# Attention on one Trainium2 core: the weights times the values in float32 on two column groups, and U^T x of the token mixing once per batch

## The chip, the cores and the metric

The kernel runs on one core of one Trainium2 chip. Its time is the device time of the whole program in microseconds (us). Five engines work side by side, each with a queue of its own that runs in order: TensorE (PE in the profile, with PEld for the loading of its weights), VectorE (DVE), ScalarE (ACT), GpSimd (POOL) and SyncE (SP, which here only issues DMAs). The kernel before takes 675.28 us, the median of three runs (675.28 to 675.33).

## The reference

Three stages, all in float32. Only the first two bear on the change.

```
q, k, v: (2, 8, 768, 64)   batch, heads, tokens, head dimension
mask   = q_assign[:, :, :, None] == k_assign[:, :, None, :]      # nearest of 16 centroids
scores = where(mask, q k^T / 8, -1e9)
attn   = exp(scores - max) / sum                                 # (768 x 768) per head
x      = attn @ v, heads side by side                            # (2, 768, 512)

h  = x^T @ U @ V            # U: 768 x 32, V: 32 x 768: mixes the tokens
u  = x + h^T
x  = u + relu(u @ w_ch1) @ w_ch2                                 # 512 -> 2048 -> 512
out = gated convolution block (512 -> 1024 -> 512)
```

## The kernel before

**Attention.** There are 2 x 8 heads of 6 row tiles of 128 tokens: 96 tiles, n = 0 to 95. `step(n)` (L666) writes out by hand what each engine does in one step; the order of the calls is the order in the queues, since the schedule is manual. In a step, three tiles are in work at once:

- PE: `s_mm(n + 2)` makes the scores of tile n + 2, 128 x 768, in PSUM (`sc`, L369 and L380, four matmuls). Then `pv_mm` (L431), then `t_mm(n)` transposes the finished weights `e` of tile n in six 128 x 128 blocks (`tr`, L407) into two PSUM tiles of three blocks.
- ACT: `t_hi(n - 1)` (L416) copies both PSUM tiles of the step before into SBUF as `ph`, rounded to the shorter format float32r. Then `s_exp(n + 1)` (L398) takes the exponential and the row sums.
- DVE: `t_lo(n - 1)` (L420) subtracts `ph` from the PSUM tile: the remainder `pl`, in float32r too. Then `s_max(n + 2)` (L386) copies the scores, scaled, to SBUF and takes the row extreme on the way.

So the weights stand in SBUF as a sum of two float32r parts. The values do too: `split_v` (L120, on POOL) puts the rounded part and the remainder of v side by side in 128 columns, `vt`. `pv_mm` takes groups of three tiles (384 columns) and, for each of the six blocks k of keys, multiplies `vt` by `ph` and by `pl`: 12 matmuls a group, four in each step. The product's upper 64 rows belong to v's rounded part, the lower 64 to its remainder.

At the end of a group, ACT copies the product out (`asb`, L440), PE turns it back in three transposes (`at`, L447), ACT copies that (`ats`, L453), POOL adds the two halves (L457) and multiplies each tile by the reciprocal of its sums (L461) into `X`.

**What limits how far engines run ahead.** The PSUM tiles `tr`, `at`, `mt`, `mu`, `mx`, `sim` and `simw` share one pool of three buffers (`ps_t`); the scores have two (`ps_s`). `t_mm(n)` needs the buffers that DVE's L420 gives back; `s_mm(n + 4)` needs the scores that the exponential of tile n + 2 has read.

**Mixing.** As soon as two heads of a batch are done, `mix_t` (L584) multiplies their 128 columns of `X` by U^T: six float32 matmuls with U three times side by side (`u3`, 96 columns), since the next product `mu` (L602) wants three copies, with float32r rounding and remainder. That is 8 calls in all. Then `mix_u` adds V^T times it and `mix_x` (L614) transposes for the following stage. These jobs stand in a list, and one is taken in certain steps of a pair of heads.

**Beside it** run, per pair of heads, the choice of centroids (`simw` L231, `sim`, `oht`), the conversion of weights for the later stages (`wx`, `wb`, `wh`, `wl` on DVE, ACT and POOL), and the loads. `simw` is of interest below: four float32 matmuls with 32 weight columns each, which write to the four quarters of the same PSUM tile's partitions (L231).

After step 95 the feed-forward blocks begin (L739 on), with the last of the attention and of the mixing between their matmuls.

Of the kernel before, what the change touches and what calls it, by code (L numbers as in the profile page):

```python
# [12 lines left out]
F32 = mybir.dt.float32  # L16
# [8 lines left out]
P = 128  # L25
# [6 lines left out]
def tile_kernel(ctx: ExitStack, tc: tile.TileContext, qk, vv, cen, u_w, v_w, w1, w2, win, wout, conv, out):  # L32
# [80 lines left out]
        nc.gpsimd.dma_start(out=ab[0:D, 1 - j], in_=qk[b, h, :, 1 - j])  # L113

    def load_v(b, p):
        rv = a_v.tile([P, 2, NT, D], F32, tag="rv", name="rv", bufs=1)
        nc.sync.dma_start(out=rv, in_=vv[b, p])
        return rv
# [232 lines left out]


    NQ = B * H * NT
    NHALF = NQ // 3
# [37 lines left out]
    def s_exp(n):  # L392
        ps = st.pop(("s", n))
        nb = st.pop(("nb", n))
        if n % 3 == 0:
            st["sum", n // 3] = a_s.tile([P, 3], F32, tag="sum", name="sum")
        e = st["e", n]
        nc.scalar.activation(e, ps[:, :, 0:HS], AF.Exp, scale=SCALE, bias=nb, accum_out=st["sum", n // 3][:, n % 3:n % 3 + 1])  # L398

    NK = NT // 2  # L400

# [8 lines left out]
    def t_hi(n, i):  # L410
        if n % 3 == 0 and i == 0:
            st["pt", n // 3] = (
                a_pt.tile([P, NT, 3, P], F32R, tag="ph", name="ph"),
                a_pt.tile([P, NT, 3, P], F32R, tag="pl", name="pl"),
            )
# [6 lines left out]
    def pv_mm(g, part):  # L422
        b, h, _ = head_of(3 * g)
        vt = vts[b, h // 2]
        if part == 0:
            st["pv", g] = ps_pv.tile([P, HS], F32, tag="pv", name="pv")
        acc = st["pv", g]
        hi, lo = st["pt", g]
        for k in range(2 * part, 2 * part + 2):
            for i, m in enumerate((hi, lo)):  # L430
                nc.tensor.matmul(  # L431
                    acc, vt[:, h % 2, k, :], m[:, k].rearrange("p a b -> p (a b)"),
                    start=(k == 0 and i == 0), stop=(k == NT - 1 and i == 1),
                )
# [7 lines left out]

    def fin_t(g):
        asb = st.pop(("asb", g))
        pt = ps_t.tile([P, 3, 2, D], F32, tag="t", name="at")
        for t in range(3):
            nc.tensor.transpose(pt[:, t].rearrange("p a d -> p (a d)"), asb[:, t * P:(t + 1) * P], identf)  # L447
        st["at", g] = pt

    def fin_x(g):  # L450
        b, h, t0 = head_of(3 * g)
        at = a_e.tile([P, 3, 2, D], F32, tag="ats", name="ats", bufs=2)
        nc.scalar.copy(at, st.pop(("at", g)))  # L453
        sm = st.pop(("sum", g))
        rs = a_s.tile([P, 3, 1], F32, tag="rs", name="rs")
        nc.vector.reciprocal(rs[:, :, 0], sm)
        nc.gpsimd.tensor_add(at[:, :, 0], at[:, :, 0], at[:, :, 1])  # L457
        if h == 0 and t0 == 0:
            X[b] = xp.tile([P, NT, DM], F32, tag="x", name="x")
        for i in range(3):  # L460
            nc.gpsimd.tensor_tensor(  # L461
                out=X[b][:, t0 + i, h * D:(h + 1) * D], in0=at[:, i, 0],
                in1=rs[:, i].to_broadcast([P, D]), op=ALU.mult,
            )

# [83 lines left out]


    load_ops(0, 0, 1)
    rv0 = load_v(0, 0)
    first_pair()
    sims(0, 1, range(2))


    u3 = mixc.tile([P, NT, 3, R], F32, name="u3")
    v3 = mixc.tile([3 * R, S], F32R, name="v3")  # L560
    cw = const.tile([P, NF2, 3], F32, name="cw")

    def put_u(x):
        for i in range(3):
            nc.gpsimd.tensor_copy(u3[:, :, i, :], x.rearrange("p (t r) -> p t r", t=NT))

    def put_v(o, x):
        nc.scalar.copy(v3[:, o:o + HS], x)
# [12 lines left out]
    mixing = []  # L581
    later = []

    def mix_t(b, p):  # L584
        cs = slice(p * P, (p + 1) * P)

        def mm():
            pt = ps_t.tile([3 * R, P], F32, tag="t", name="mt")
# [39 lines left out]
    def mix_rest(b):  # L628
        for t in range(NT):
            mixing.append(mix_u(b, t))  # L630
        for t in range(NT):
            (mixing if b * NT + t < TG or b > 0 else later).append(mix_x(b, t))

    def prep(n):

        pair, s = divmod(n, 2 * NT)
        nxt = pair + 1
        if nxt < B * NP:
            b, p = divmod(nxt, NP)
            for part, at in enumerate((3, 3, 4, 4, 5) if nxt > 1 else (0, 0, 1, 2, 3)):  # L640
                if s == at and (nxt > 1 or part > 1):
                    sims_onehot(b, p, part)
            if s == 1:
                split_ops(b, p, 0, nc.gpsimd)
            elif s == 3:
                load_ops(b, p, 1)
            elif s == 4:
                st["rv"] = load_v(b, p)
            elif s == 7:
                split_ops(b, p, 1, nc.gpsimd)  # L650
            elif s == 8:
                split_v(b, p, st.pop("rv"))
# [12 lines left out]

    def step(n):  # L666
        pair, s = divmod(n, 2 * NT)
        mix = None
        if s == 8 and pair > 0 and n < NQ:
            b, p = divmod(pair - 1, NP)  # L670
            mixing.insert(0, mix_t(b, p))
            if p == NP - 1:
                mix_rest(b)
# [10 lines left out]
        if 0 <= g - 1 < NHALF and r == 0:  # L684
            fin_t(g - 1)
        elif mixing and (s in (0, 8, 9, 11) or pair == B * NP - 1):
            mix = mixing.pop(0)
            got = mix[0]()
        if s == 2 and n < NQ and 1 < pair + 1 < B * NP:
            sims_wide(*divmod(pair + 1, NP))  # L690
        if s == 3 and n < NQ and 1 < pair + 1 < B * NP:
            sims_turn(*divmod(pair + 1, NP))
        if 0 <= n < NQ:
            t_mm(n)
        if 0 <= n - 1 < NQ:
            for i in range(2):
                t_hi(n - 1, i)
                t_lo(n - 1, i)
        if 0 <= n + 1 < NQ:
            s_exp(n + 1)  # L700
        if s == 2 and n < NQ and 1 < pair + 1 < B * NP:
            sims_copy(*divmod(pair + 1, NP))
        if n == -1:
            split_first(1, "q")
            load_ops(0, 1, 0)
            split_ops(0, 0, 1, nc.gpsimd)
            split_v(0, 0, rv0)
# [103 lines left out]
    for n in range(NQ - 1, NQ + 6):  # L811
# [169 lines left out]
```

## Time and profile before

| | us |
|---|---|
| median of the runs | 675.28 |
| the profiled execution | 675.47 |
| its span, first to last instruction | 673.7 |
| PE busy | 657.8 (98%) |
| DVE busy | 455.9 (68%) |
| ACT busy | 371.2 (55%) |
| POOL busy | 292.9 (43%) |

The profiled execution is 1.77 us longer than its span. PE is busy nearly everywhere, but the matmul records overlap: each one lasts longer than the distance to the next, so PE's work has to be read from the distance between starts. DVE and ACT are busy in the first third of the span, which is the attention, and less so after it.

### The profile page before, as it was taken

To read this page: it belongs to the slowest core of one execution; us is meant where nothing else is said; L and a number is where in the kernel's file an instruction comes from. 1 tells how busy PE (TensorE), PEld (TensorE's weight loads), DVE (VectorE), ACT (ScalarE), POOL (GpSimd) and SP (SyncE) were. 2 spreads that over 40 slices of the span, in tenths; PEclk is the share of its full clock that TensorE was granted. 3 is DMA by queue.
4 is the path that set the end of the run, shared out by engine and by line. 5 is a ranking of instruction groups with operands and counts; after the bars stand their busy time and mean duration, and the time that the engine had idled before them with its cause. 6 is when DMAs were issued, how large, how long until landed. Compare 5 with 4: busy or idle time off the path is not lost.

```text
span 673.7 us, 10313 instructions
## 1 busy us (share of the span) xinstructions
PE 657.8 (98%) x3708; PEld 571.3 (85%) x3708; DVE 455.9 (68%) x840; ACT 371.2 (55%) x749; POOL 292.9 (43%) x384
## 2 busy tenths in 40 slices
PE   9899999999999999999999999999999999999997
PEld 6799999988888898889888888888877888888886
DVE  6998999899999897388524778773267536542400
ACT  5888989887878896324312333332134356753511
POOL 4886767666565533244420333331044643422300
PEclk9999999999999999999999999999999999999999
DMA  8584565455463202113201443432023000010111
GB/s 189 132 175 101 118 148 128 131 116 145 87 157 74 75 1 74 53 62 120 71 1 53 136 133 126 128 114 64 0 63 125 1 1 1 0 33 17 47 48 47
DMA packets 19587, 55.48 MB, mean 82 GB/s; under 512 B 3312, under 2 KB 7024, under 8 KB 19536
## 3 DMA queue, kind: packets, MB, share of 16 engines
q1 hardware_dynamic: 15936, 40.08, 20.0%
q0 software_dynamic: 3600, 14.75, 10.9%
q8 instruction: 29, 0.48, 0.3%
q14 instruction: 22, 0.18, 0.1%
HBM read 50.19 MB, written 3.15 MB: 79 GB/s over the span
## 4 chain that ended last, share of the span: by engine, by line
PE 81%; DVE 10%; ACT 3%; issue 3%; POOL 2%; DMA 1%; ACTq 0%; POOLq 0%; DVEq 0%
PE g L870 10%; PE pv L431 8%; PE tr L407 8%; PE h L747 6%; PE h L748 6%; PE h L749 6%; PE a L764 5%; PE a L763 5%; PE a L765 5%; PE sc L369 4%; PE sc L380 4%; PE po L905 3%; PE po L904 3%; PE po L906 3%; DVE pl L420 2%
## 5 line engine op out<-in xcount | busy, mean ns | idle before, releaser
L545 POOL TENSOR_TENSOR wl<-wx,wh 128x512 fp32r<-128x512 f32 x48 | 63.0, 1314 | 116.7 <-ACT wh L544 116.4
L420 DVE TENSOR_TENSOR pl<-tr,ph 128x384 fp32r<-128x384 f32 x192 | 97.3, 547 | 12.1 <-ACT ph L416 12.0
L407 PE MATMUL tr<-identf,e 128*128 128x128 f32 x576 | 85.3, 277 | 6.9 <-DVE pl L420 4.6
L386 DVE TENSOR_SCALAR_CACHE_REDUCE e<-sc 128x768 f32<-128x768 f32 x96 | 90.6, 945 | 0.3 <-PE sc L380 0.3
L398 ACT ACTIVATE e<-sc,nb 128x768 f32<-128x768 f32 x96 | 88.2, 918 | 4.4 <-DVE e L386 4.2
L752 ACT ACTIVATE rh<-h 128x512 fp32r<-128x512 f32 (+1 forms) x52 | 29.3, 563 | 110.7 <-PE h L749 110.7
L416 ACT CAST ph<-tr 128x384 fp32r<-128x384 f32 x192 | 84.2, 485 | 9.9 <-PE tr L407 9.1
L753 DVE SCALAR_TENSOR_TENSOR rl<-h,rh 128x512 fp32r<-128x512 f32 (+1 forms) x52 | 33.6, 647 | 82.3 <-ACT rh L752 82.2
L407 PEld LDWEIGHTS tr<-identf,e 128*128 128x128 f32 x576 | 65.5, 140 | 20.9 <-DVE pl L420 12.5
L747 PE MATMUL h<-uh,wh 128*128 128x512 f32 (+1 forms) x208 | 78.1, 375 | 1.6 <-DVE rl L753 1.6
L763 PE MATMUL a<-rh,wh 128*128 128x512 f32 (+1 forms) x208 | 78.1, 375 | 0.5 <-DVE xa L779 0.5
L764 PE MATMUL a<-rl,wh 128*128 128x512 f32 (+1 forms) x208 | 77.8, 374 | 0.5 <-DVE rl L753 0.3
L765 PE MATMUL a<-rh,wl 128*128 128x512 f32 (+1 forms) x208 | 77.6, 373 | 0.0
L748 PE MATMUL h<-ul,wh 128*128 128x512 f32 (+1 forms) x208 | 77.5, 373 | 0.0
L749 PE MATMUL h<-uh,wl 128*128 128x512 f32 (+1 forms) x208 | 77.5, 373 | 0.0
L431 PE MATMUL pv<-ph,vt 128*128 128x384 f32 x192 | 65.7, 342 | 0.7 <-POOL vt L123 0.5
L431 PE MATMUL pv<-pl,vt 128*128 128x384 f32 x192 | 64.9, 338 | 0.0
L544 ACT CAST wh<-wx 128x512 fp32r<-128x512 f32 x48 | 29.8, 620 | 59.3 <-DVE wx L498 59.2
L887 POOL TENSOR_TENSOR h<-h,cv 128x768 f32<-128x768 f32 x16 | 29.6, 1852 | 64.5 <-ACT cv L886 64.5
L369 PE MATMUL sc<-ab 128*128 128x384 f32 x192 | 57.0, 378 | 0.3 <-ACT e L398 0.3
L494 DVE SCALAR_TENSOR_TENSOR wx<-wb,wx 128x512 int32<-128x512 int32 (+3 forms) x52 | 47.1, 905 | 12.1 <-ACT wb L485 9.5
L457 POOL TENSOR_TENSOR ats<-ats 128x192 f32<-128x192 f32 x32 | 20.6, 644 | 72.3 <-ACT ats L453 65.2
(144 smaller groups left out, 1494.9 us busy)
## 6 DMA issues: line engine op xcount, KB each, us to landing
raw<-in_w_dram SPq DMA_DIRECT2D x32, 512.0 KB, 3.7
cd<-in_qk_dram POOLq DMA_DIRECT2D x15, 384.0 KB, 4.2
ab<-in_qk_dram POOLq DMA_DIRECT2D x15, 384.0 KB, 5.4
raw<-in_win_dram SPq DMA_DIRECT2D x8, 512.0 KB, 3.7
raw<-in_wout_dram SPq DMA_DIRECT2D x8, 512.0 KB, 3.7
rv<-in_vv_dram SPq DMA_DIRECT2D x8, 384.0 KB, 3.0
out_dram<-o SPq DMA_DIRECT2D x24, 128.0 KB, 1.8
ab<-in_qk_dram POOLq DMA_DIRECT2D x15, 192.0 KB, 5.6
```

What stands on the lines that cost most here:

```text
L386: nc.vector.tensor_scalar(out=e, in0=ps[:, :, 0:HS], scalar1=-SCALE, scalar2=3e38, op0=ALU.mult, op1=ALU.min, accum_out=nb,)
L398: nc.scalar.activation(e, ps[:, :, 0:HS], AF.Exp, scale=SCALE, bias=nb, accum_out=st["sum", n // 3][:, n % 3:n % 3 + 1])
L407: nc.tensor.transpose(pt[:, k, :], e[:, i, k * P:(k + 1) * P], identf)
L416: nc.scalar.copy(st["pt", n // 3][0][:, i * NK:(i + 1) * NK, n % 3, :], st["t", n, i])
L420: nc.vector.tensor_sub(lo, st.pop(("t", n, i)), hi)
L431: nc.tensor.matmul(acc, vt[:, h % 2, k, :], m[:, k].rearrange("p a b -> p (a b)"), start=(k == 0 and i == 0), stop=(k == NT - 1 and i == 1),)
L747: nc.tensor.matmul(ph, wh[:, k, ws], uh[g][:, k, ts], start=(k == 0), stop=False)
L748: nc.tensor.matmul(ph, wh[:, k, ws], ul[g][:, k, ts], start=False, stop=False)
L749: nc.tensor.matmul(ph, wl[:, k, ws], uh[g][:, k, ts], start=False, stop=(k == ND - 1))
L763: nc.tensor.matmul(accs[d][:, 0:n], wh[:, i, ds_], rh, start=(f == 0), stop=False)
L764: nc.tensor.matmul(accs[d][:, 0:n], wh[:, i, ds_], rl, start=False, stop=False)
L765: nc.tensor.matmul(accs[d][:, 0:n], wl[:, i, ds_], rh, start=False, stop=(f == NH - 1))
```

## The change

The weights are no longer split. `t_out` replaces `t_hi` and `t_lo`: ACT copies the first PSUM tile of a step into SBUF as float32 (`pt`), DVE the second. The values are used as they are loaded, in float32, so that `split_v` goes.

`pv_mm` takes a whole head (six tiles) and runs in float32: for each block k two matmuls, each with the same 64 columns of values as weights, one over tiles 0 to 2 (384 columns) into PSUM partitions 0 to 63, one over tiles 3 to 5 into partitions 64 to 127. They are issued two k at a time, in every second step of the next head (`PLAN`); in the last head in three steps in a row. The end of a group now comes once a head: one copy of the product by ACT, three transposes, one reciprocal and one multiplication on DVE straight from PSUM into `X`. The copy `ats` and POOL's additions and multiplications go.

U is held once, in 32 columns. `mix_t` is called once a batch, when all heads are done: for each of the six tiles, four matmuls over four blocks of 128 columns of `X`, into the four quarters of one PSUM tile's partitions. Its evacuation makes the three copies: per block, ACT copies twice and DVE subtracts once, on 32 partitions each. The steps in which a mixing job may be taken are moved to 0, 4, 8 and 10.

```diff
-    def split_v(b, p, rv):
-        vt = a_v.tile([P, 2, NT, 2 * D], F32R, tag="vt", name="vt")
-        nc.gpsimd.tensor_copy(vt[:, :, :, 0:D], rv)
-        nc.gpsimd.tensor_sub(vt[:, :, :, D:2 * D], rv, vt[:, :, :, 0:D])
-        vts[b, p] = vt
...
-        nc.scalar.copy(st["pt", n // 3][0][:, i * NK:(i + 1) * NK, n % 3, :], st["t", n, i])
-
-    def t_lo(n, i):
-        hi, lo = (t[:, i * NK:(i + 1) * NK, n % 3, :] for t in st["pt", n // 3])
-        nc.vector.tensor_sub(lo, st.pop(("t", n, i)), hi)
+    def t_out(n, i):
+        if n % NT == 0 and i == 0:
+            st["pt", n // NT] = a_pt.tile([P, NT, NT, P], F32, tag="pt", name="pt")
+        to = st["pt", n // NT][:, i * NK:(i + 1) * NK, n % NT, :]
+        (nc.scalar.copy if i == 0 else nc.vector.tensor_copy)(to, st.pop(("t", n, i)))
+
+    def pv_mm(g, k):
...
+        for i in range(2):
+            nc.tensor.matmul(
+                acc[i * D:(i + 1) * D], vts[b, h // 2][:, h % 2, k], pt[:, k, i * NK:(i + 1) * NK].rearrange("p a b -> p (a b)"),
+                start=(k == 0), stop=(k == NT - 1),
             )
...
-        at = a_e.tile([P, 3, 2, D], F32, tag="ats", name="ats", bufs=2)
-        nc.scalar.copy(at, st.pop(("at", g)))
...
-        nc.gpsimd.tensor_add(at[:, :, 0], at[:, :, 0], at[:, :, 1])
...
-            nc.gpsimd.tensor_tensor(
-                out=X[b][:, t0 + i, h * D:(h + 1) * D], in0=at[:, i, 0],
-                in1=rs[:, i].to_broadcast([P, D]), op=ALU.mult,
-            )
+        nc.vector.tensor_tensor(
+            out=X[b][:, :, h * D:(h + 1) * D].rearrange("p (a t) d -> p a t d", a=2),
+            in0=st.pop(("at", g)).rearrange("p t a d -> p a t d"),
+            in1=rs.to_broadcast([P, 2, NK, D]), op=ALU.mult,
+        )
...
-                nc.tensor.matmul(pt, u3[:, t].rearrange("p a r -> p (a r)"), X[b][:, t, cs], start=(t == 0), stop=(t == NT - 1))
+                for c in range(ND):
+                    nc.tensor.matmul(
+                        pt[c * R:(c + 1) * R], uw[:, t], X[b][:, t, c * P:(c + 1) * P], start=(t == 0), stop=(t == NT - 1))
...
-            nc.scalar.copy(tts[b][:, cs], pt)
-            nc.vector.tensor_sub(tts[b][R:2 * R, cs], pt[R:2 * R], tts[b][R:2 * R, cs])
+            for c in range(ND):
+                src, cs = pt[c * R:(c + 1) * R], slice(c * P, (c + 1) * P)
+                nc.scalar.copy(tts[b][0:R, cs], src)
+                nc.vector.tensor_sub(tts[b][R:2 * R, cs], src, tts[b][0:R, cs])
+                nc.scalar.copy(tts[b][2 * R:3 * R, cs], src)
...
+    PLAN = ({2 * k: (2 * k, 2 * k + 1) for k in range(NK)}, NT - 2), ({k: (2 * k, 2 * k + 1) for k in range(NK)}, NK - 1)
+    MIX_AT = (0, 4, 8, 10)
...
-        g, r = divmod(n - 4, 3)
-        if 0 <= g < NHALF:
-            pv_mm(g, r)
+        g, r = divmod(n - NT - 1, NT)
+        ks, last = PLAN[g == NHEAD - 1]
+        if 0 <= g < NHEAD:
+            for k in ks.get(r, ()):
+                pv_mm(g, k)
```

The order of PE's queue in the middle of the attention, before: every step has its four matmuls `pv`, and every third step three transposes `at`.

```order
L447 MATMUL at<-identf,asb 128x128 x3
L407 MATMUL tr<-identf,e 128x128 x6
L369 MATMUL sc<-ab 128x384 x2
L380 MATMUL sc<-cd 128x384 x2
L431 MATMUL pv<-ph,vt 128x384
L431 MATMUL pv<-pl,vt 128x384
L431 MATMUL pv<-ph,vt 128x384
L431 MATMUL pv<-pl,vt 128x384
L407 MATMUL tr<-identf,e 128x128 x6
L369 MATMUL sc<-ab 128x384 x2
L380 MATMUL sc<-cd 128x384 x2
L431 MATMUL pv<-ph,vt 128x384
```

The same place in the changed kernel (line numbers there are its own). `rv` is the values as loaded; a product stands with 64 rows because each writes half of the partitions.

```order
L418 MATMUL pv<-pt,rv 64x384 x4
L402 MATMUL tr<-identf,e 128x128 x6
L364 MATMUL sc<-ab 128x384 x2
L375 MATMUL sc<-cd 128x384 x2
L402 MATMUL tr<-identf,e 128x128 x6
L364 MATMUL sc<-ab 128x384 x2
L375 MATMUL sc<-cd 128x384 x2
L418 MATMUL pv<-pt,rv 64x384 x4
L434 MATMUL at<-identf,asb 128x128 x3
L402 MATMUL tr<-identf,e 128x128 x6
L364 MATMUL sc<-ab 128x384 x2
L375 MATMUL sc<-cd 128x384 x2
```

Steps with four `pv` matmuls and steps without any now take turns, and `at` comes once in six steps.

ACT's queue in the attention, before: two copies `ph` a step ahead of the exponential, with the copies `asb` and `ats` every third step.

```order
L440 COPY asb<-pv 128x384
L416 CAST ph<-tr 128x3x128 x2
L398 ACTIVATE e,sum<-sc,nb 128x768
L453 COPY ats<-at 128x384
L416 CAST ph<-tr 128x3x128 x2
L398 ACTIVATE e,sum<-sc,nb 128x768
```

In the changed kernel, around the one evacuation of the mixing's first product in batch 0 (`tt`, L579 and L581):

```order
L409 COPY pt<-tr 128x3x128
L393 ACTIVATE e,sum<-sc,nb 128x768
L579 CAST tt_284<-mt 32x128
L581 CAST tt_284<-mt 32x128
L579 CAST tt_284<-mt 32x128
L581 CAST tt_284<-mt 32x128
L579 CAST tt_284<-mt 32x128
L581 CAST tt_284<-mt 32x128
L579 CAST tt_284<-mt 32x128
L581 CAST tt_284<-mt 32x128
L409 COPY pt<-tr 128x3x128
L393 ACTIVATE e,sum<-sc,nb 128x768
```

One copy a step is left ahead of the exponential; the eight small copies stand in a row between two steps, twice in the kernel.

## Rows read from the trace of the kernel before

**Rows 1.** The page: busy time by engine, and three lines of its 40 slices.

```profile
PE 657.8 (98%) x3708; PEld 571.3 (85%) x3708; DVE 455.9 (68%) x840; ACT 371.2 (55%) x749; POOL 292.9 (43%) x384
...
DVE  6998999899999897388524778773267536542400
ACT  5888989887878896324312333332134356753511
...
PEclk9999999999999999999999999999999999999999
```

**Rows 2.** Busy time by stretch: attention, its tail, the rest (stretch, length, busy).

```profile
17.00:261.80 244.80, 236.90 (x1626) 217.07 (x1625) 225.53 (x491) 207.21 (x476) 159.87 (x250) 1.00 0.49 111
261.80:320.00 58.20, 56.43 (x361) 50.80 (x360) 41.55 (x66) 21.16 (x43) 22.81 (x25) 1.00 0.25 80
```

**Rows 3.** Waits, 17 to 261.8 us: who for whom, total, times, longest.

```profile
PEld tr L407 <- DVE pl L420: 12.5, 31, 1.1
DVE pl L420 <- ACT ph L416: 12.0, 29, 1.0
...
PEld tr L407 <- ACT ats L453: 3.8, 7, 1.0
```

**Rows 4.** Timeline of PE around one `simw`: start, duration, engine, line, out<-in.

```profile
46.73 0.49 PE L447 MATMUL at<-identf,asb 128*128 128x128 f32 x3
47.05 0.82 PE L407 MATMUL tr<-identf,e 128*128 128x128 f32 x6
...
48.41 0.34 PE L431 MATMUL pv<-ph,vt 128*128 128x384 f32 x1
...
48.95 0.34 PE L431 MATMUL pv<-pl,vt 128*128 128x384 f32 x1
49.22 0.51 PE L231 MATMUL simw<-rq,cbq 128*32 128x384 f32 x1
49.23 0.51 PE L231 MATMUL simw<-rk,cbk 128*32 128x384 f32 x1
49.23 0.51 PE L231 MATMUL simw<-rq,cbq 128*32 128x384 f32 x1
49.24 0.51 PE L231 MATMUL simw<-rk,cbk 128*32 128x384 f32 x1
49.56 0.49 PE L231 MATMUL simw<-rq,cbq 128*32 128x384 f32 x1
...
50.00 0.87 PE L407 MATMUL tr<-identf,e 128*128 128x128 f32 x6
50.63 0.59 PE L369 MATMUL sc<-ab 128*128 128x384 f32 x2
```

**Rows 5.** Timeline of PE around one `mt` and the step behind it.

```profile
155.83 1.47 PE L590 MATMUL mt<-x,u 128*96 128x128 f32 x12
157.14 0.82 PE L407 MATMUL tr<-identf,e 128*128 128x128 f32 x6
157.71 0.59 PE L369 MATMUL sc<-ab 128*128 128x384 f32 x2
```

**Rows 6.** Groups by line and form: count, busy, mean ns, idle before.

```profile
L420 DVE TENSOR_TENSOR pl<-tr,ph 128x384 fp32r<-128x384 f32 x192 | 97.3, 547 | 12.1 <-ACT ph L416 12.0
L386 DVE TENSOR_SCALAR_CACHE_REDUCE e<-sc 128x768 f32<-128x768 f32 x96 | 90.6, 945 | 0.3 <-PE sc L380 0.3
L398 ACT ACTIVATE e<-sc,nb 128x768 f32<-128x768 f32 x96 | 88.2, 918 | 4.4 <-DVE e L386 4.2
L407 PE MATMUL tr<-identf,e 128*128 128x128 f32 x576 | 85.3, 277 | 6.9 <-DVE pl L420 4.6 <-ACT ats L453 2.1
L416 ACT CAST ph<-tr 128x384 fp32r<-128x384 f32 x192 | 84.2, 485 | 9.9 <-PE tr L407 9.1
...
L407 PEld LDWEIGHTS tr<-identf,e 128*128 128x128 f32 x576 | 65.5, 140 | 20.9 <-DVE pl L420 12.5 <-ACT ats L453 3.8 <-issue 1.9
```

**Rows 7.** Timeline of ACT at that `mt`: its evacuation.

```profile
157.34 0.26 ACT L594 CAST tt<-mt 96x128 fp32r<-96x128 f32 x1 [1.12 <-PE mt L590]
```

More of the change, by code (lines that the diff above doesn't have):

```diff
@@ L115, in load_v @@
     def load_v(b, p):
-        rv = a_v.tile([P, 2, NT, D], F32, tag="rv", name="rv", bufs=1)
-        nc.sync.dma_start(out=rv, in_=vv[b, p])
-        return rv
-    def split_v(b, p, rv):
-        vt = a_v.tile([P, 2, NT, 2 * D], F32R, tag="vt", name="vt")
-        nc.gpsimd.tensor_copy(vt[:, :, :, 0:D], rv)
-        nc.gpsimd.tensor_sub(vt[:, :, :, D:2 * D], rv, vt[:, :, :, 0:D])
-        vts[b, p] = vt
+        vts[b, p] = a_v.tile([P, 2, NT, D], F32, tag="rv", name="rv")
+        nc.sync.dma_start(out=vts[b, p], in_=vv[b, p])
     def split_ops(b, p, j, eng):
@@ L353, in tile_kernel @@
     NQ = B * H * NT
-    NHALF = NQ // 3
+    NHEAD = B * H
     st = {}
@@ L394, in s_exp @@
         nb = st.pop(("nb", n))
-        if n % 3 == 0:
-            st["sum", n // 3] = a_s.tile([P, 3], F32, tag="sum", name="sum")
+        if n % NT == 0:
+            st["sum", n // NT] = a_s.tile([P, NT], F32, tag="sum", name="sum", bufs=4)
         e = st["e", n]
-        nc.scalar.activation(e, ps[:, :, 0:HS], AF.Exp, scale=SCALE, bias=nb, accum_out=st["sum", n // 3][:, n % 3:n % 3 + 1])
+        nc.scalar.activation(e, ps[:, :, 0:HS], AF.Exp, scale=SCALE, bias=nb, accum_out=st["sum", n // NT][:, n % NT:n % NT + 1])
     NK = NT // 2
@@ L408, in t_mm @@
             st["t", n, i] = pt
[L410 to L414, printed above, removed]
-            )
-        nc.scalar.copy(st["pt", n // 3][0][:, i * NK:(i + 1) * NK, n % 3, :], st["t", n, i])
-    def t_lo(n, i):
-        hi, lo = (t[:, i * NK:(i + 1) * NK, n % 3, :] for t in st["pt", n // 3])
-        nc.vector.tensor_sub(lo, st.pop(("t", n, i)), hi)
[L422 to L433, printed above, removed]
-                )
-        if part == 2:
+    def t_out(n, i):
[4 more added lines that the diff above has]
+    def pv_mm(g, k):
+        b, h, _ = head_of(NT * g)
+        if k == 0:
+            st["pv", g] = ps_pv.tile([P, HS], F32, tag="pv", name="pv")
+        acc, pt = st["pv", g], st["pt", g]
+        for i in range(2):
+            nc.tensor.matmul(
+                acc[i * D:(i + 1) * D], vts[b, h // 2][:, h % 2, k], pt[:, k, i * NK:(i + 1) * NK].rearrange("p a b -> p (a b)"),
+                start=(k == 0), stop=(k == NT - 1),
+            )
+        if k == NT - 1:
             st.pop(("pt", g))
@@ L444, in fin_t @@
         asb = st.pop(("asb", g))
-        pt = ps_t.tile([P, 3, 2, D], F32, tag="t", name="at")
-        for t in range(3):
+        pt = ps_t.tile([P, NK, 2, D], F32, tag="t", name="at")
+        for t in range(NK):
             nc.tensor.transpose(pt[:, t].rearrange("p a d -> p (a d)"), asb[:, t * P:(t + 1) * P], identf)
@@ L450, in fin_x @@
     def fin_x(g):
-        b, h, t0 = head_of(3 * g)
-        at = a_e.tile([P, 3, 2, D], F32, tag="ats", name="ats", bufs=2)
-        nc.scalar.copy(at, st.pop(("at", g)))
-        sm = st.pop(("sum", g))
-        rs = a_s.tile([P, 3, 1], F32, tag="rs", name="rs")
-        nc.vector.reciprocal(rs[:, :, 0], sm)
-        nc.gpsimd.tensor_add(at[:, :, 0], at[:, :, 0], at[:, :, 1])
-        if h == 0 and t0 == 0:
-            X[b] = xp.tile([P, NT, DM], F32, tag="x", name="x")
-        for i in range(3):
-            nc.gpsimd.tensor_tensor(
-                out=X[b][:, t0 + i, h * D:(h + 1) * D], in0=at[:, i, 0],
-                in1=rs[:, i].to_broadcast([P, D]), op=ALU.mult,
-            )
+        b, h, _ = head_of(NT * g)
+        rs = a_s.tile([P, 2, NK, 1], F32, tag="rs", name="rs")
+        nc.vector.reciprocal(rs.rearrange("p a t o -> p (a t o)"), st.pop(("sum", g)))
+        if h == 0:
+            X[b] = xp.tile([P, NT, DM], F32, tag="x", name="x")
+        nc.vector.tensor_tensor(
[3 more added lines that the diff above has]
+        )
     chunks = {}
@@ L553, in tile_kernel @@
     load_ops(0, 0, 1)
-    rv0 = load_v(0, 0)
+    load_v(0, 0)
     first_pair()
     sims(0, 1, range(2))
-    u3 = mixc.tile([P, NT, 3, R], F32, name="u3")
+    uw = mixc.tile([P, NT, R], F32, name="uw")
     v3 = mixc.tile([3 * R, S], F32R, name="v3")
@@ L563, in put_u @@
     def put_u(x):
-        for i in range(3):
-            nc.gpsimd.tensor_copy(u3[:, :, i, :], x.rearrange("p (t r) -> p t r", t=NT))
+        nc.gpsimd.tensor_copy(uw.rearrange("p t r -> p (t r)"), x)
     def put_v(o, x):
@@ L582, in tile_kernel, with mix_t @@
     later = []
-    def mix_t(b, p):
-        cs = slice(p * P, (p + 1) * P)
+    def mix_t(b):
         def mm():
-            pt = ps_t.tile([3 * R, P], F32, tag="t", name="mt")
+            pt = ps_t.tile([P, P], F32, tag="t", name="mt")
             for t in range(NT):
-                nc.tensor.matmul(pt, u3[:, t].rearrange("p a r -> p (a r)"), X[b][:, t, cs], start=(t == 0), stop=(t == NT - 1))
+                for c in range(ND):
+                    nc.tensor.matmul(
+                        pt[c * R:(c + 1) * R], uw[:, t], X[b][:, t, c * P:(c + 1) * P], start=(t == 0), stop=(t == NT - 1))
             return pt
         def evac(pt):
-            nc.scalar.copy(tts[b][:, cs], pt)
-            nc.vector.tensor_sub(tts[b][R:2 * R, cs], pt[R:2 * R], tts[b][R:2 * R, cs])
+            for c in range(ND):
[3 more added lines that the diff above has]
+                nc.scalar.copy(tts[b][2 * R:3 * R, cs], src)
         return mm, evac
@@ L646, in prep @@
                 load_ops(b, p, 1)
-            elif s == 4:
-                st["rv"] = load_v(b, p)
             elif s == 7:
@@ L651, in prep @@
             elif s == 8:
-                split_v(b, p, st.pop("rv"))
+                load_v(b, p)
             if s == (6 if nxt > 1 else 5):
@@ L670, in step @@
             b, p = divmod(pair - 1, NP)
-            mixing.insert(0, mix_t(b, p))
             if p == NP - 1:
+                mixing.append(mix_t(b))
                 mix_rest(b)
@@ L680, in step @@
             s_mm(n + 2)
-        g, r = divmod(n - 4, 3)
-        if 0 <= g < NHALF:
-            pv_mm(g, r)
-        if 0 <= g - 1 < NHALF and r == 0:
-            fin_t(g - 1)
-        elif mixing and (s in (0, 8, 9, 11) or pair == B * NP - 1):
+        g, r = divmod(n - NT - 1, NT)
[3 more added lines that the diff above has]
+                pv_mm(g, k)
+        done = g - 1 if r == 0 else g if g == NHEAD - 1 and r == last + 1 else -1
+        if 0 <= done < NHEAD - (r == 0):
+            fin_t(done)
+        elif mixing and (s in MIX_AT or pair == B * NP - 1):
             mix = mixing.pop(0)
@@ L696, in step @@
             for i in range(2):
-                t_hi(n - 1, i)
-                t_lo(n - 1, i)
+                t_out(n - 1, i)
         if 0 <= n + 1 < NQ:
@@ L706, in step @@
             split_ops(0, 0, 1, nc.gpsimd)
-            split_v(0, 0, rv0)
         if n == 0:
@@ L712, in step @@
             s_max(n + 2)
-        if 0 <= g < NHALF and r == 0:
+        if 0 <= g < NHEAD and r == 0:
             sm = st["sum", g]
             nc.gpsimd.tensor_scalar(out=sm, in0=sm, scalar1=1e-9, scalar2=None, op0=ALU.add)
-        if 0 <= g < NHALF and r == 2:
+        if 0 <= g < NHEAD and r == last:
             fin_a(g)
-        if 0 <= g - 1 < NHALF and r == 0:
-            fin_x(g - 1)
+        if 0 <= done < NHEAD - (r == 0):
+            fin_x(done)
         if mix:
@@ L816, in tile_kernel @@
             pump(FLOW)
-    mixing.append(mix_t(B - 1, NP - 1))
+    mixing.append(mix_t(B - 1))
     mix_rest(B - 1)
```

## The prediction

> **What bounds the kernel now.** I read the page first: PE is busy 98% of the span, at full clock in all 40 slices, and DVE and ACT are near nine tenths in the first third only [rows 1]. So the attention is the one stretch where a change on any of three engines can move the time, and later stretches have PE alone. The table by stretch confirms it: between the first transposes at 17.0 and the first feed-forward matmul at 261.8, DVE is busy 225.5 of 244.8 us (92%) and ACT 207.2 (85%), while in the tail DVE falls to 71% [rows 2]. There are 96 steps in that stretch, 2.55 us each.
>
> The waits say what holds PE up there [rows 3]. The weight loads of the transposes `tr` wait 12.5 us in 31 places for DVE's subtraction L420, and 3.8 us in 7 places for ACT's copy `ats`: both give back a buffer of the shared PSUM pool. DVE in turn waits 12.0 us for ACT's copy `ph`, since the remainder can't be formed before the rounded part. A load lasts 0.14 us [rows 6] and normally runs that far ahead of its matmul, so 38 places hide about 5.3 us, and 16.3 - 5.3 = 11 us stood on PE. The rest of the stretch is PE's own work. Two sums follow: what PE has to do, and how much of those 11 us goes.
>
> **PE's work, part by part.** Starts, not durations, count. Before, the four `pv` matmuls of a step are 0.18 us apart (48.41 to 48.95 is three of them), 0.72 a step, 96 x 0.72 = 69.1 us [rows 4].
>
> The new product isn't in the trace, but a near relative is: `simw` also runs in float32, over 384 columns, with its outputs in different parts of the partitions. Its four matmuls stand as eight records. Four start within 0.02 us of each other at 49.22, the other four 0.34 us later at 49.56 [rows 4]. I read this as: a float32 matmul takes two passes of 0.34 us each, and matmuls on different column groups run at the same time. From the last `pv` before it (48.95) to the first `sc` after it (50.63) is 1.68 us; without it this would be 0.18 for the `pv` and 0.57 from `tr` to `sc` [rows 5], 0.75 together. So `simw` costs 0.93 us, 0.68 of it two passes and 0.25 going into this layout of the array and out of it.
>
> A burst of the changed kernel is two blocks k with two matmuls each: four passes deep if the two column groups overlap, 4 x 0.34 + 0.25 = 1.61, or 1.57 with passes of 0.33; I take 1.60. There are 3 bursts in each of 16 heads: 48 x 1.60 = 76.8 us, which is 7.7 us more than before. Bounds: with no price for the change of layout, 48 x 1.32 = 63.4 (5.7 less than before); with no overlap at all, 48 x (8 x 0.33 + 0.25) = 139. The trace has groups of 32 columns only, so that 64 behave alike is the nearest row and not a proof.
>
> In the Trainium skill, TensorEngine Tiling (Array Packing), Key Properties says that changing the tiling mode drains the TensorE; the 0.25 us above is what this trace gives for one change in and out. By that rule a layout that is entered 48 times more has a price however well its groups overlap, which speaks against the change.
>
> The transposes `at` take 0.32 us for three (46.73 to 47.05 [rows 4]) and come 16 times instead of 32: -5.1 us. `mt` takes 1.31 us, twelve passes of 0.109 (155.83 to 157.14 [rows 5]), eight times: 10.5 us. After, it comes twice; 24 matmuls on four column groups are again twelve passes deep, 1.31 + 0.25 = 1.56, 3.1 us together: -7.4 us. PE's work: 7.7 - 5.1 - 7.4 = -4.8 us.
>
> **The waits.** DVE loses 97.3 us of subtractions [rows 6], gets 96 plain copies of the same size (0.485 us by ACT's copy of such a tile, 0.547 at most by its own old operation [rows 6]; I take 0.485, 47 us), and 16 multiplications of about 0.55: roughly -42 us. Over a stretch of some 233 us it would be busy 183 us, 79%. ACT loses half of its copies (-42 us [rows 6]), `ats` and half of `asb`, and falls to some 62%. The two halves of a transposed tile are now copied at the same time by two engines and not one after the other by both, so the buffers come back sooner, and the chain ACT before DVE is gone. POOL's work on v and on the products goes, but POOL was not on PE's path but for the first values; I cost that at nothing.
>
> What is late next is a ring through the exponential. In a step with a burst: `sc` 0.71, the burst 1.60, three transposes 0.33, ACT's copy 0.485, the exponential of tile n + 2, 0.918 [rows 6], whose scores buffer the next `sc` with a burst behind it needs: 4.04 us and three hand-overs, about 4.25. PE's own two steps are 2 x 1.36 (47.05 to 48.41 [rows 4]) + 1.60 = 4.32 us. The ring is just shorter. So it costs little as long as nothing is added, and DVE's conversions and one-hot work will still be late now and then. Of the 11 us I let 3.5 stay: -7.5 us. Bounds: 0 (all stay, under the new name) and -11.
>
> **The evacuation of `mt`.** One copy of 0.26 us [rows 7] becomes eight on ACT, all ahead of the next step's copy and exponential: 2.1 us instead of 0.26, twice in the kernel, so up to 3.6 us later. ACT has slack in most steps; the first sits in a step without a burst. In the tail, feed-forward matmuls stand in front of `mu`. I take +1.5 us, bounds 0 and +3.6.
>
> **Sum.** -4.8 - 7.5 + 1.5 = -10.8 us. The profiled execution took 675.47, so 664.7; the median of the runs is 0.2 lower: 664.5 us. After 261.8 nothing else changes but that the last head's three bursts (4.8 us) follow in place of four sets of `pv` (2.9), counted above.
>
> **Rivals.**
>
> *Passes in strict order.* The two passes of one matmul stand one behind the other in program order. If the array can't start the second group's first pass before the first group's second, each burst is one pass longer: 48 x 0.34 = 16.3 us, and `mt`, with four groups, needs 4 x 0.109 instead of 2 x 0.109 per tile, 2 x 6 x 0.218 = 2.6 us. With 3.5 us of waits swallowed: 664.5 + 16.3 + 2.6 - 3.5 = 680, slower. It decides from 0.23 us a burst on, where the 10.8 are gone. Against it: in `simw` the third matmul starts at 49.23, before any second pass [rows 4]. For it: the starts are the profile's reading, and `simw` has a distinct group for each matmul, while a burst comes back to the same group. In the Trainium skill, TensorE: Matmul & The Clock Gate, What overlaps and what doesn't, matmuls are said to start and end strictly in program order; by that rule this rival holds, and rows 4 can be reconciled with it only if the passes are issued interleaved. I give it 0.10.
>
> *No overlap of 64-wide groups.* Then PE does 139 us in bursts, 70 more; `mt` 2 x (48 x 0.109 + 0.25) = 11.0, 0.5 more; `at` -5.1; all 11 us of waits vanish: 675.3 + 70 + 0.5 - 5.1 - 11 + 1.5 = 731 us. For it only that no row shows 64. 0.06.
>
> *The ring takes over.* Steps with a burst (2.96 us on PE) and without (1.36) alternate, and a step of 1.36 is shorter than ACT's copy and exponential (1.40). If hand-overs and late row extremes make the ring 4.55 and not 4.25, PE waits 0.23 in every pair of steps: 48 x 0.23 = 11 us come back, 675. For it: the margin is 0.07 us. Against it: mixing products, `oht` and `simw` stand in steps without a burst and give the ring room in many pairs. 0.14.
>
> *Better than forecast*: no wait stays and the change of layout is partly hidden under other work, 48 x 0.1: 664.5 - 3.5 - 4.8 = 656. 0.04.
>
> **How the numbers follow.** The forecast, with 0.66, has a range of its own of 658 to 671, by its waits (4 to either side) and the price of the layout. The measurement can't tell less than 0.2%, 1.4 us. Faster: 0.66 + 0.04 + half of the ring's case, 0.06 = 0.76. Same: 0.04, from the ring. Slower: 0.10 + 0.06 + 0.04 of the ring = 0.20. The range 655 to 678 takes in the better case and the ring's, and leaves out the two in which the groups don't overlap as read.
>
> **What would show it.** Right: in the profile after, bursts of eight `pv` records, in pairs of starts a few hundredths apart, pairs about 0.33 apart, and 1.6 us from the end of `sc` to the next `tr` beyond the usual distance; attention of about 233 us; `tr` waiting a few us in all; `mt` 1.6 us. The strict order would show as bursts near 1.95; no overlap as 2.9. The ring would show as `sc` waiting for the exponential at the start of steps with a burst. Wrong for other reasons: DVE's copy far above 0.55, or the 261.8 to 320 stretch getting longer.

## The result, and the profile after

The changed kernel takes 667.81 us (median of 4 runs, 665.61 to 668.33), the kernel before 675.28 (4 runs, 675.25 to 675.33): a ratio of 0.9883, with a 95% interval of 0.987 to 0.9896. That is 7.5 us faster, where 10.8 were forecast; the range of 655 to 678 holds it. In the experiments, a gain over the kernel before is worked out from the ratio (7.9 us for this change), a distance between two other kernels from their medians. The profiled execution of after took 668.33 us, with a span of 666.3.

The page after, busy time and two lines of the 40 slices, answers to [rows 1]:

```profile
PE 648.6 (97%) x3660; PEld 511.5 (77%) x3660; DVE 428.1 (64%) x744; ACT 319.9 (48%) x613; POOL 221.3 (33%) x222
...
DVE  6988788887889875388326868873177445643400
ACT  5765666666666773334213343331135367753511
```

The first feed-forward matmul now starts at 250.6 and not at 261.8. Busy time by stretch (stretch, length, then PE, PEld, DVE, ACT, POOL), against [rows 2]:

```profile
17.00:250.60 233.60, 224.94 (x1530) 158.69 (x1528) 197.86 (x392) 154.69 (x334) 91.07 (x96) 1.00 0.52 117
250.60:320.00 69.40, 67.15 (x447) 56.19 (x446) 47.67 (x80) 25.50 (x53) 26.39 (x24) 1.00 0.21 69
```

The attention is 11.2 us shorter. ACT fell from 85% to 66% of it, DVE from 92% to 85% only. The span is 7.4 us shorter, so 3.8 us came back behind the attention.

The bursts, on PE's timeline (start, duration, engine, line, operation, out<-in; eight records of four matmuls in one row). The first two rows end a step without a burst, the next four are a step with one, and behind it comes a step without:

```profile
110.76 0.52 PE L375 MATMUL sc<-cd 80*128 80x384 f32 x2
111.12 0.82 PE L402 MATMUL tr<-identf,e 128*128 128x128 f32 x6
111.70 0.62 PE L364 MATMUL sc<-ab 128*128 128x384 f32 x2
112.16 0.52 PE L375 MATMUL sc<-cd 80*128 80x384 f32 x2
112.61 1.51 PE L418 MATMUL pv<-pt,rv 128*64 128x384 f32 x8
114.05 0.88 PE L402 MATMUL tr<-identf,e 128*128 128x128 f32 x6
114.68 0.59 PE L364 MATMUL sc<-ab 128*128 128x384 f32 x2
115.11 0.51 PE L375 MATMUL sc<-cd 80*128 80x384 f32 x2
115.47 0.82 PE L402 MATMUL tr<-identf,e 128*128 128x128 f32 x6
117.22 0.49 PE L273 MATMUL oht<-identb,oh 128*64 128x128 bf16 x6 [0.94 <-DVE pt L409]
```

From the second pair of `sc` to the next first pair it is 111.70 - 110.76 = 0.94 us without a burst and 114.68 - 112.16 = 2.52 with one. A burst costs 1.58 us; 1.60 was forecast from `simw` [rows 4]. The last row shows what was not forecast: the one-hot transposes `oht` wait 0.94 us. In the table of waits (17 to 250.6 us: who for whom, total, times, longest), against [rows 3]:

```profile
PE oht L273 <- DVE pt L409: 5.5, 6, 0.9
...
PEld tr L402 <- DVE e L381: 4.2, 7, 0.6
PEld L273 <- DVE oh L265: 4.1, 6, 0.7
PEld tr L402 <- ACT e L393: 3.8, 6, 0.6
PEld tr L402 <- DVE pt L409: 3.1, 6, 0.8
```

The old waits for the subtraction L420 and for `ats` are gone. Of the new ones, the loads' waits of 0.6 us at `tr` mostly stand behind a burst, whoever is named: there the first load starts together with its matmul (both at 114.05), elsewhere 0.18 us ahead of it (115.29 and 115.47). They are in the 1.58 us of a burst already. The 5.5 us before `oht`, in six pairs of heads, are PE's own.

The last of DVE's one-hot work are `eq` (L261) and `oh` (L265), each with two inputs in SBUF. DVE and POOL at that place, one fence each, with the same columns:

```profile
112.36 0.35 DVE L261 TENSOR_TENSOR eq<-eq,iota 128x384 bf16<-128x384 bf16 x1
112.75 0.55 DVE L263 TENSOR_REDUCE m<-eq 128x24 bf16<-128x384 bf16 x1
114.55 2.15 DVE L265 TENSOR_TENSOR oh<-eq,m 128x384 bf16<-128x384 bf16 x1
...
116.62 0.55 DVE L409 COPY pt<-tr 128x384 f32<-128x384 f32 x1
```

```profile
112.47 1.92 POOL L125 TENSOR_TENSOR ab<-rk,cd 64x768 fp32r<-64x768 f32 x1 [0.42 <-DMA cd<-in_qk_dram]
114.46 1.82 POOL L126 TENSOR_TENSOR ab<-rq,ab 64x768 fp32r<-64x768 f32 x1
```

DVE's last one-hot operation starts 0.09 us after POOL's subtraction and ends 0.42 us after it, at 116.70. DVE's copy `pt` stands behind it in DVE's queue, and that copy is what `oht` waits for: it gives back a buffer of the shared PSUM pool. In the kernel before, the same one-hot operation lasted 0.55 us at this pair:

```profile
118.81 0.55 DVE L270 TENSOR_TENSOR oh<-eq,m 128x384 bf16<-128x384 bf16 x1
```

The subtraction of `rk` and `cd` that stands at 112.47 after the change came only 5.6 us behind it there. POOL's queue had the products of the group in front of it, and these waited 5.00 us for ACT's copy `ats`:

```profile
123.46 0.59 POOL L457 TENSOR_TENSOR ats<-ats 128x192 f32<-128x192 f32 x1 [5.00 <-ACT ats L453]
...
124.93 1.81 POOL L130 TENSOR_TENSOR ab<-rk,cd 64x768 fp32r<-64x768 f32 x1
```

Over the attention the mean of `oh` went from 604 to 1292 ns, that of `eq` from 570 to 1054. Of the six pairs, three have a long `oh` and the other three a long `eq`:

```profile
L265 DVE TENSOR_TENSOR oh<-eq,m 128x384 bf16<-128x384 bf16 x7 | 9.0, 1292 | 0.0
L261 DVE TENSOR_TENSOR eq<-eq,iota 128x384 bf16<-128x384 bf16 x7 | 7.4, 1054 | 0.0
```

In the Trainium skill, SBUF — State Buffer, SBUF: two separate sides says that DVE and POOL share one pair of ports as an exclusive lock, which a DVE operation with two inputs in SBUF needs against a POOL operation that reads SBUF: who starts first has it for the whole instruction, and the other stands still. The rows agree: 2.15 us for an operation of 0.55. In the run of the changed kernel again, below, DVE is first at this pair, by 0.08 us (115.23 and 115.31): its operation lasts 0.55 us and POOL's subtraction 2.15 instead of 1.82.

### The profile page after: what moved, and what is told of

It reads as the page before. It is cut to its first block, busy times and chain, and to the rows that moved or that the text cites. A ratio compares the mean times of both kernels' runs of the same rounds, so it can differ in the third digit from the quotient of the medians.

```text
span 666.3 us, 9744 instructions
## 1 busy us (share of the span) xinstructions
PE 648.6 (97%) x3660; PEld 511.5 (77%) x3660; DVE 428.1 (64%) x744; ACT 319.9 (48%) x613; POOL 221.3 (33%) x222
## 4 chain that ended last, share of the span: by engine, by line
PE 82%; DVE 10%; issue 3%; ACT 2%; POOL 1%; DMA 0%; DVEq 0%; ACTq 0%; POOLq 0%
PE g L860 10%; PE pv L418 9%; PE tr L402 7%; PE h L737 6%; PE h L739 6%; PE h L738 6%; PE a L753 6%; PE a L755 5%; PE a L754 5%; PE sc L364 4%; PE sc L375 4%; PE po L894 3%; PE po L895 3%; PE po L896 3%; DVE e L381 2%
## 5 line engine op out<-in xcount | busy, mean ns | idle before, releaser
L393 ACT ACTIVATE e<-sc,nb 128x768 f32<-128x768 f32 x96 | 86.8, 905 | 21.8 <-DVE e L381 21.5
L402 PE MATMUL tr<-identf,e 128*128 128x128 f32 x576 | 81.2, 276 | 1.2 <-ACT tt L581 0.7
L418 PE MATMUL pv<-pt,rv 128*64 128x384 f32 x384 | 72.5, 499 | 0.0
L409 ACT COPY pt<-tr 128x384 f32<-128x384 f32 x96 | 46.0, 479 | 41.1 <-PE tr L402 41.0
L409 DVE COPY pt<-tr 128x384 f32<-128x384 f32 x96 | 52.8, 551 | 14.3 <-PE tr L402 13.6
L477 DVE SCALAR_TENSOR_TENSOR wx<-wb,wx 128x512 int32<-128x512 int32 (+3 forms) x52 | 47.9, 921 | 11.6 <-ACT wb L468 9.6
L375 PE MATMUL sc<-cd 80*128 80x384 f32 x192 | 49.5, 339 | 0.0
L737 PEld LDWEIGHTS h<-uh,wh 128*128 128x128 f32 x208 | 39.2, 188 | 9.3 <-DVE rl L743 1.9
```

Source lines behind the costliest of these rows:

```text
L409: (nc.scalar.copy if i == 0 else nc.vector.tensor_copy)(to, st.pop(("t", n, i)))
L418: nc.tensor.matmul(acc[i * D:(i + 1) * D], vts[b, h // 2][:, h % 2, k], pt[:, k, i * NK:(i + 1) * NK].rearrange("p a b -> p (a b)"), start ...
L737: nc.tensor.matmul(ph, wh[:, k, ws], uh[g][:, k, ts], start=(k == 0), stop=False)
```

## The experiments

**The two halves of the change.** First the products alone, with the mixing as before: the changed kernel with these lines put back (and the copies of U and the evacuation that belong to them).

```diff
-                mixing.append(mix_t(b))
+            mixing.insert(0, mix_t(b, p))
```

> The changed kernel with the mixing's first product as before (U three times side by side, eight calls). Theory A (PE's own work and DVE's lateness set the attention; the mixing gave PE 7.4 us and cost a serial evacuation): the products alone bring -7.4 + 1.5 less than the whole, so 673 us, 5 to 6 above the changed kernel, with each burst still 1.60 us. Rival B (the mixing's part cost as much in its evacuation as it gave): 668, the same as the changed kernel.

669.53 us, ratio 0.9919 (0.9892 to 0.9946), 5.5 us faster than before. It lies between the two theories, nearer to B.

Then the mixing alone: the kernel before, with the new `mix_t` and `uw`.

> The kernel before with the mixing's new first product only (once a batch, four column groups). Theory A: 10.5 us of PE work become 3.1, the evacuation gives 1.5 back: 669 to 671. Rival B: within 1 us of 675.3. Rival C (DVE bounds the old attention, so PE's saving is idle time): 674 to 675.

671.11 us, ratio 0.9926 (0.990 to 0.9953), 5.0 us faster, about as theory A had it. Two of its four runs, with a mean granted clock of 0.999, took 669.1 and 669.9 us; the other two, at 0.992 and 0.994, took 672.3 and 672.5. The profile is one of the latter: from 158.8 to 165.7 us the granted clock is 0.50, which is 1.2 GHz, and just before PE had waited 1.41 us at `mu` for the evacuation of `mt`. The two halves together would be 10.5 us; by the same reckoning the whole change brings 7.9 and, run again below, 8.8 (0.9883 and 0.9869). The intervals are too wide to make much of the difference.

**How many bursts a head.** The plan of the bursts alone is changed, first to five a head:

```diff
-({2 * k: (2 * k, 2 * k + 1) for k in range(NK)}, NT - 2)
+({0: (0,), 1: (1,), 2: (2,), 3: (3,), 4: (4, 5)}, 4)
```

> The changed kernel with five bursts a head (four of one block, one of two) in place of three of two. Theory A (each change of the array's layout costs PE 0.25 us): 15 heads x 2 more bursts x 0.25 = +7.5 us, 675. Rival B (uneven steps and the ring through the exponential hold PE up more than the layout does): the steps are even now, so at most 668.

670.61 us, ratio 0.9925 (0.9909 to 0.9942): 2.8 us slower than the changed kernel, between A and B. The rows of PE show why both are half right. A step with a burst of one block:

```profile
122.66 0.52 PE L375 MATMUL sc<-cd 80*128 80x384 f32 x2
123.11 0.87 PE L418 MATMUL pv<-pt,rv 128*64 128x384 f32 x4
123.90 0.33 PE L402 MATMUL tr<-identf,e 128*128 128x128 f32 x1
```

From `sc` to `tr` it is 1.24 us here, 1.89 with two blocks (112.16 to 114.05 above) and 0.36 without (115.11 to 115.47). So a block is 0.65 us, two passes of 0.325, and a burst has 0.23 us on top, which I read as the price of the layout. Thirty more bursts are 7 us. But the waits before `oht` fell to 1.3 us in 2 places, so that 4 us of it came back.

Then two bursts of three blocks:

```diff
-({2 * k: (2 * k, 2 * k + 1) for k in range(NK)}, NT - 2)
+({0: (0, 1, 2), 3: (3, 4, 5)}, 3)
-    MIX_AT = (0, 4, 8, 10)
+    MIX_AT = (0, 5, 8, 11)
```

> The changed kernel with two bursts of three blocks a head, mixing jobs in steps 0, 5, 8 and 11. Theory A: 15 x 0.25 = 3.8 us less, 664. Rival B (uneven steps): two steps without a burst in a row run at ACT's pace of 1.6 us and not PE's 1.36, 15 x 4 x 0.25 = 15 us of waits against the 3.8 saved: 675 or more.

671.48 us, ratio 0.993 (0.9905 to 0.9955), 3.7 us slower than three bursts although PE has less to do. Theory A, 3.8 us faster, is out; B had the sign and too large a size. But uneven steps are not the only thing that differs. The mixing's jobs stand in other steps, and the transposes wait 2.1 us for the evacuation of `mt` instead of 0.7; that wait ends at 155.76, and from 157.4 to 160.8 us the granted clock is 0.50 (1.2 GHz). Three of the four runs have a mean clock of 0.994 to 0.997, and the one at 0.999 took 669.08 us. So this run alone does not show what uneven steps cost.

**Does the overlap hang on the order of the queue?** The four matmuls of a burst in another order, both blocks of one column group first:

```diff
-            for k in ks.get(r, ()):
-                pv_mm(g, k)
+            for i in range(2):
+                for k in ks.get(r, ()):
+                    pv_mm(g, k, (i,))
```

> The changed kernel with the four matmuls of a burst in another order: both blocks of the first half (column group 0), then both of the second half (group 1). Theory A (each column group takes its passes from a queue of its own, whatever stands between): no change, 667 to 668, bursts of 1.6 us. Rival B (passes start in program order, and the overlap needs neighbours in the queue to be of different groups): the second group starts three passes late, 7 passes deep and not 4: 48 x 3 x 0.33 = 47 us more, less some 6 us of waits, 708.

668.22 us (two runs, 666.36 and 670.09), ratio 0.989 (0.9853 to 0.9926), and the burst is as long as before:

```profile
113.23 1.52 PE L418 MATMUL pv<-pt,rv 128*64 128x384 f32 x8
114.68 0.55 PE L402 MATMUL tr<-identf,e 128*128 128x128 f32 x3
```

1.45 us, against 1.44 in the changed kernel. The second record of the burst starts 13 ns behind the first, where it was 7 in the changed kernel; that fits the first group's other matmul, which now stands between the two in the queue and starts only later, at 113.61 or after. So the order written does not matter. The strict order that was a rival of the prediction would make this burst seven passes deep, and the rule of the Trainium skill that the prediction names beside that rival does not hold for these matmuls.

**Both halves on one column group.** The products of both halves go to the same rows, but for the first block:

```diff
-                acc[i * D:(i + 1) * D], ...
-                start=(k == 0), stop=(k == NT - 1),
+                acc[i * D * (k == 0):i * D * (k == 0) + D], ...
+                start=(k == 0), stop=(i == 1 and k in (0, NT - 1)),
```

> The changed kernel with both halves' products in the first half's rows, so on one column group (only at the first block the second half still has its own rows; the output rows of tiles 3 to 5 are left out, those of 0 to 2 are mixed up). Theory A (the overlap of column groups is what makes the float32 product affordable): a burst of two blocks is eight passes deep, 8 x 0.325 + 0.28 = 2.9 in place of 1.6; for the last two bursts of each head 32 x 1.3 = 42, for the first with one block overlapped 16 x 0.65 = 10; 52 us more, less 6 of waits: 713. Rival B (the weights' loading hides the second group anyway, and passes are not what counts): under 680.

711.21 us, ratio 1.0526 (1.0505 to 1.0547), 44 us above the changed kernel on the same chip, close to theory A's 713. The later two bursts of a head are eight passes deep, the first one six:

```profile
110.64 2.79 PE L418 MATMUL pv<-pt,rv 128*64 128x384 f32 x8
113.36 0.88 PE L402 MATMUL tr<-identf,e 128*128 128x128 f32 x6
...
116.27 2.15 PE L418 MATMUL pv<-pt,rv 128*64 128x384 f32 x8
```

2.72 us and not 1.44. With the overlap gone the change would have been a loss of 36 us.

**POOL's subtractions in pieces.** What held DVE's one-hot work up is made short, not moved:

```diff
-        eng.tensor_sub(ab[0:D, j], lo[0:D], cd[0:D, j])
+        for c0 in range(0, S, S // 4):
+            c = slice(c0, c0 + S // 4)
+            eng.tensor_sub(ab[0:D, j, c], lo[0:D, c], cd[0:D, j, c])
```

and the second subtraction alike.

> The changed kernel with each of POOL's subtractions for the operands (1.85 us) cut into four of 192 columns. In the changed kernel DVE's one-hot operations over bf16 last up to 2.15 us when they begin under such a subtraction, and PE waits 0.9 us for them in six pairs. Theory A (DVE stands still until POOL's instruction ends): those operations are back near 0.6 us, PE's wait before `oht` goes, 3 to 5 us: 663 to 665. Rival B (the operations are long for another reason, or the wait moves elsewhere): 667 to 669.

661.02 us (660.74 to 661.19), ratio 0.9783 (0.9768 to 0.9797): 6.1 us below the changed kernel on the same chip, and the fastest of all. DVE and POOL at the place shown above, one fence each:

```profile
111.56 0.56 DVE L269 TENSOR_TENSOR oh<-eq,m 128x384 bf16<-128x384 bf16 x1
```

```profile
109.95 2.62 POOL L127 TENSOR_TENSOR ab<-rk,cd 64x192 fp32r<-64x192 f32 x4 [0.90 <-DMA cd<-in_qk_dram]
112.64 2.25 POOL L130 TENSOR_TENSOR ab<-rq,ab 64x192 fp32r<-64x192 f32 x4
```

The one-hot operation starts 0.05 us ahead of the fourth piece and lasts 0.56 us; that piece, at 111.61, then takes 0.96 us, where the others take 0.59. Where a piece has started first, `oh` lasts up to 0.80. The wait before `oht` is 0.3 us in one place. The attention:

```profile
17.00:243.30 226.30, 224.04 (x1530) 158.30 (x1527) 187.90 (x392) 154.25 (x335) 107.16 (x186) 1.00 0.55 121
```

226.3 us, 7.3 less than in the changed kernel, with POOL busy 16 us longer. The spread of the runs went too: 0.45 us, where the changed kernel has 2.7 in the first set and 1.5 in the one that follows.

The changed kernel again, on the same chip:

> The changed kernel again, on the same chip as the three others, as what they are compared with: 667 to 668.

667.09 us, ratio 0.9869 (0.9852 to 0.9886). In its profile, three pairs and not six wait before `oht` (2.8 us): a tenth of a microsecond decides who is first, so the collision falls differently from run to run.

**Is the collision old?** The kernel before with the same pieces:

> The kernel before with POOL's subtractions for the operands in four pieces each. Theory A (the collision of DVE and POOL is old, and held the kernel before up as well; there DVE is the busier engine): 2 to 5 us faster, 670 to 673. Rival B (the change made the collision: its POOL, freed of the products, now runs these subtractions under the one-hot work): within 1 us of 675.4.

673.88 us, ratio 0.998 (0.997 to 0.9989): 1.4 us, between the two and nearer to B. The same cut is worth 6.1 us after the change and 1.4 before it. Then with the subtraction of the values cut as well:

> The kernel before with POOL's subtractions for the operands and for the values (1.85 us each, 31 and 8 of them) in four pieces each. Theory A (part of what the change gained came from dropping the values' subtraction on POOL, under which DVE's weight conversion stood still, 1.78 us at 160.59 for an operation of 0.42): 671 to 672.5, below the 673.9 of the operands' pieces alone. Rival B (only the one-hot operations hurt, since PE waits for those alone): 673.5 to 674.5.

672.69 us, ratio 0.9956 (0.9942 to 0.997), 3.0 us, just above theory A's range and well below B's. So cutting that subtraction on POOL, which the change removes, gave 1.0 us by the medians and 1.6 by the ratios, whose intervals touch; that it cost PE time before the change is likely and not more. In the trace of before, DVE's conversion and POOL's subtraction of the values, one fence each:

```profile
160.59 1.78 DVE L490 TENSOR_SCALAR wx<-raw 128x512 int32<-128x512 int32 x1
```

```profile
160.24 1.85 POOL L123 TENSOR_TENSOR vt<-rv,vt 128x768 fp32r<-128x768 f32 x1
```

They end within 0.3 us of each other; the same conversion has a median of 0.42 us.

**Pieces and two bursts.**

> The changed kernel with POOL's subtractions in pieces and two bursts of three blocks a head. Theory A (two bursts were slower only through the collision): 3.8 us less than with the pieces alone, 657. Rival B (the steps without a burst run at ACT's and DVE's pace): 661 to 665, no better than three bursts.

668.03 us, ratio 0.9893 (0.987 to 0.9915), 7 us slower than three bursts with pieces and above both forecasts. Two runs with a mean clock of 1.00 took 666.6 and 666.9 us, the other two, at 0.994, 669.1 and 670.0; so 5.7 us of the 7 are there at full clock. Two waits in its profile, over the attention; with three bursts and pieces they are 0.7 and 0.4:

```profile
PE tr L406 <- ACT tt L585: 2.1, 1, 2.1
PEld sc L368 <- ACT e L397: 1.8, 5, 0.4
```

The first, 1.4 us more, is the mixing's evacuation, which this plan puts in another step. The rest, and the 3.5 us that 15 changes of layout less should give, went into the steps without a burst. The third of three such steps in a row, up to the next scores:

```profile
127.71 0.82 PE L406 MATMUL tr<-identf,e 128*128 128x128 f32 x6
128.63 0.62 PE L368 MATMUL sc<-ab 128*128 128x384 f32 x2
```

It needs 0.92 us from `tr` to `sc` and not 0.57 [rows 5], and the load of this `sc` waits 0.34 us for the exponential L397. That is the ring of the prediction's third rival. It is named in 5 places only; what holds the other steps up was not found.

**The evacuation of the mixing's first product.** With the pieces, ACT's four second copies behind all first copies and subtractions:

> The changed kernel with POOL's subtractions in pieces and the evacuation of the mixing's first product in another order: per block one copy by ACT and DVE's subtraction, then the four second copies. In the changed kernel ACT and DVE take turns block by block and the chain lasts 3.5 us (275.3 to 278.8). Theory A: it becomes 2.1 us, `mu` and the transposes behind it wait 0.6 and 1.3 us less, 659 to 660. Rival B (covered by other work): 661.

661.18 us, ratio 0.979 (0.9773 to 0.9806), no change. It doesn't tell the theories apart, because the chain did not get shorter: ACT's next first copy waits for DVE's subtraction of the block before, although it reads other partitions of the tile. Why it waits was not tried.

```profile
268.21 0.26 ACT L583 CAST tt<-mt 32x128 fp32r<-32x128 f32 x1 [0.88 <-PE mt L576]
268.81 0.26 ACT L583 CAST tt<-mt 32x128 fp32r<-32x128 f32 x1 [0.35 <-DVE tt L584]
...
270.65 1.06 ACT L587 CAST tt<-mt 32x128 fp32r<-32x128 f32 x4 [0.36 <-DVE tt L584]
```

It lasts 3.5 us from 268.21 to 271.71, as long as in the other order.

## Why the prediction was right, and where it was short

*The float32 product on two column groups* was right in mechanism and size: 1.58 us a burst against 1.60, a pass of 0.325, 0.23 on top of the passes against 0.25. That `simw` with its 32 columns stood for 64 held. The two rivals on overlap are out: one group alone costs 44 us more, and the order in the queue has no effect.

*The mixing's saving* held: 5.0 us alone (3.2 to 6.8 by the interval), against 7.4 - 1.5 = 5.9 forecast.

*The waits* are the term that was mis-sized: 7.5 us were to go, and about 4 went. That is nearly the whole shortfall. "Of the 11 us I let 3.5 stay" was wrong at both ends, as an estimate from PE's rows shows. I add up by how much the distance between the starts of two neighbouring groups of matmuls exceeds the usual (median) distance of that kind: about 14 us over the attention before, 10 after, and 4 with the pieces. So more stood on PE than the 11 that I took as the bound, and about 10 stayed. The two errors partly cancelled. The terms say nearly the same. PE's -4.8, of which 2.7 for the last head and 0.2 for `mt` are paid in the tail (see below), is -7.7 in the attention; with half the evacuation, +0.8, the old waits would leave 237.9 us. It took 233.6, 4.3 less, and with the pieces 226.3, 11.6 less.

The reason is in a sentence of mine: POOL's work goes, "I cost that at nothing". It doesn't cost nothing. With the products gone from its queue, the subtraction that used to wait behind them starts as soon as its operands land (L125 waits for a DMA above), and that is now under the one-hot operations, with PE waiting for what stands behind these on DVE. The same cut of the subtractions gives 6.1 us after the change and 1.4 before it. DVE is busy 197.9 us, where some 183 were forecast: 6 us are its plain copies, 551 ns and not 485, and 8 the longer `eq` and `oh`.

The third rival, the ring through the exponential, had the right symptom (waits come back) and another mechanism. With pieces and three bursts, the matmuls `sc` wait 0.5 us for the exponential in all, so the margin of 0.07 us was enough; with bursts of three blocks the ring shows in a few places.

*The evacuation of `mt`* cost PE 0.7 us at `tr` in the attention and 0.6 at `mu` in the tail, 1.3 against +1.5. It lasts 3.5 us each time and not 2.1, since ACT and DVE take turns.

*The tail* came out 3.8 us longer, against 1.9 + 0.2 + 0.7 = 2.8 in the terms. Up to the first matmul `a` it is 2.8 us: the last head's three bursts replace three sets of `pv` behind the boundary (2.1 us), not four, and that is 2.7. The other 1.0 us is mostly the longer `mt` and the wait at `mu`.

## What to carry to other kernels

In this kernel it was worth pairing a float32 matmul of 64 weight columns with a second one on the other half of the output partitions: the pair took the time of one, for about a quarter of a microsecond a burst, and three bursts a head did better than five or two. When work is taken off an engine, ask not only what it no longer delays but when its remaining instructions will now run, and which engine's operations they then fall on. Long subtractions on POOL next to DVE's two-input operations were best cut here: more instructions, 16 us more POOL time, and 6 us less in all.

## What was not expected of the hardware

- DVE operations of 0.35 to 0.56 us with two bf16 inputs in SBUF last up to 2.15 us when they start under a POOL subtraction of 1.82; a reduction with one input does not (0.55 us at 112.75, inside the subtraction of 112.47). With pieces of some 0.6 us they last 0.80 at most.
- Matmuls of one column group that stand ahead of the other group's in the queue do not hold it up: a burst of eight passes, four on each group, takes 1.44 us in one order and 1.45 in the other.
- The time of DVE's plain copy of a PSUM tile of 128 x 384 (551 ns) is that of the subtraction that it replaces (547 [rows 6]); ACT's is 479.
